# Running maximum in two groups for the dispatch softmax, idle matmuls between the logits' steps, and a table turned by copies

## The chip, the cores and the metric

One core of a Trainium2 chip runs the whole program. The metric is the device time of one execution in microseconds (us); lower is better. Engines are called PE (TensorE's matmuls; PEld is its weight loads), DVE (VectorE), ACT (ScalarE), POOL (GpSimd) and SP (the queue from which nearly all DMAs are issued).

## The reference

Three stages follow one another. x has 8 batches of 3072 tokens of 256 numbers, 24576 tokens in all.

```python
def _attn_ref(x):                       # x: (8, 3072, 256)
    X = np.fft.fft(x, axis=1)
    X = np.fft.fft(X, axis=2)
    return X.real.astype(np.float32)

def _moe_ref(x, phi, w1, w2):           # x: (24576, 256), phi: (256, 32)
    logits = x @ phi
    d = np.exp(logits - logits.max(0, keepdims=True))     # dispatch softmax, over tokens
    d /= d.sum(0, keepdims=True) + 1e-09
    slot_input = d.T @ x                                  # 32 slots
    ...                                                   # 8 experts of 4 slots: relu(s @ w1) @ w2
    c = np.exp(logits - logits.max(1, keepdims=True))     # combine softmax, over slots
    c /= c.sum(1, keepdims=True) + 1e-09
    return c @ slot_out

def _moe2_ref(x, w_in, w_out, s, b):
    r = np.maximum(x @ w_in, 0.0)
    return (s * (r * r) + b) @ w_out
```

The change concerns `logits`, `d` and the sum `d.T @ x`. The maximum over tokens, one number for each of the 32 slots, only keeps the exponentials in range: any common factor of a slot's column of `exp` is divided out again by the sum below it.

## The kernel before

The program is one stream of instructions for each engine, in the order in which the Python code emits them; each engine works through its own stream in order and waits at semaphores that the framework sets. Memory that holds 1 MB blocks is cut into pages: a ring of 15, and 5 more once the first stage is over (`page`, `drop`, `more_pages`). The helper `pump` emits the next pending loads (`todo`) as soon as the count of free pages allows; on the chip SP then waits until the last reader of that page is done. `ORDER` is the order of the first loads: x blocks (`x`), second-layer weights (`w`), the logits' tables (`l`, `ltab_load`), the transform's tables (`h`, `htab_load`) and the x pages that the sum `d.T @ x` reads (`r`, `load_xr`).

The first stage projects the turned x on phi and does one part of the Fourier transform. It leaves `tt`. Then come the parts that the change touches, in this order:

- **Logits** (lines 561 to 592). 16 chunks in two halves `h` that sit in the lower and upper 64 rows. The loop runs 9 steps `st`; a step does one chunk of each half (the first and the last step one chunk only). One chunk is 8 matmuls in the code, 16 records in the trace, into a PSUM tile `lp`, of which there are six. ACT copies `lp` to `lg` (L583). DVE takes the maximum over the chunk's 16 entries of each slot out of `lp` into a column of `cm` (L585).
- **Maximum over tokens** (lines 588 to 611). DVE folds the columns of `cm` (L589, L592), PE turns the result (L598), DVE reduces it over the rows (L603) and spreads it on a diagonal (L605), PE multiplies by ones (L607), DVE copies the result to `cmb` (L608). PE runs idle matmuls on `ones` beside it (`keep_warm`, L190). Two pending steps of the second-layer weights (L216) are emitted here too, by `side_step`; the page `wo` is dropped after the last of them. `fill_stack` (L534 to L536) makes six small copies on ACT.
- **Transform of the weights** (lines 613 to 670). 16 chunks `i`. `emit_d` subtracts `cmb` from the logits (L633, odd chunks on POOL, even ones on DVE), ACT takes the exponential (L669), PE does 4 matmuls against the tables `htab_t` (L652; 8 records of 104 columns on 128 weight columns), and `h_out` copies each chunk's result to `hh` (L643), one half on ACT and the other on DVE.
- **Sum over tokens** (lines 675 to 862). For each of 14 steps PE turns `hh` (L704), multiplies by a DFT table (L712), and adds `d.T @ x` into `racc` (L727). Each part drops the x page that it has read, and `pump` loads another page there: the rest of x, then the second-layer input weights and the experts' weights w1 and w2. After that the experts run, and at some 238 us the last stage starts, which lasts to the end.

Each half of a transform table is loaded twice (L352): into rows 0 to 47 and into rows 64 to 111. `htab_clear` (L357) then clears what each copy must not hold.

Of the kernel before, what the change touches and what calls it, by code (L numbers as in the profile page):

```python
# [32 lines left out]
def tile_fft2__then__softmoe__then__act_relu2(  # L33
# [18 lines left out]
    nc = tc.nc  # L52
# [244 lines left out]
    ORDER = "xxxwxxxxxxwxxxxxxwxxxxwxrllhhrr"  # L297
# [48 lines left out]
    def htab_load(i):  # L346

        t, k = page([R, 16, 2, 4 * MH], F32, "htab_t")
        htabs.append((t, k))
        nc.gpsimd.memset(t[32:64], 0.0)  # L350
        for q in range(2):
            nc.sync.dma_start(out=t[64 * q:64 * q + M], in_=htab[:, 32 * i:32 * i + 32].rearrange("r (k q) m -> r k q m", q=2))  # L352
        dma_ready(2.5)
# [172 lines left out]
    cmb = keep.tile([P, NE], F32, name="cmb")  # L526
# [25 lines left out]
    temps = tc.alloc_tile_pool(name="temps", bufs=1, side="right")  # L552
    cm = temps.tile([R, NCH + 1, NE], F32, name="cm")
    cm1 = temps.tile([R, NE], F32, name="cm1")
    def lgf(i):
        return lg[i // 4][:, 4 * (i % 4):4 * (i % 4) + 4].rearrange("p k g e -> p (k g) e")

    with tc.tile_pool(name="ps_l", bufs=6, space=PSUM) as psl, \
            tc.tile_pool(name="ps_m", bufs=1, space=PSUM) as psm:
        mxp[:] = [psm, 1]  # L560
        done_l = 0
        for st in range(NCH // 2 + SKEW):
            halves = [(h, st - SKEW * h) for h in range(2) if 0 <= st - SKEW * h < NCH // 2]
            lps = {h: psl.tile([R, KC, NG * NE], F32, name="lp") for h, _ in halves}
            for k in range(2 * KC):
                q = P // 2 * (k % 2)
                m = M if q else P // 2
                for h, i8 in halves:
                    r = slice(64 * h, 64 * h + 64)
                    nc.tensor.matmul(  # L570
                        lps[h][q:q + m, k // 2, :], lhsT=ltabs[i8 // 4][0][r, 2 * KC * (i8 % 4) + k, 0:m],
                        rhs=tt[r, 2 * KC * i8 + k].rearrange("p b e -> p (b e)"), start=True, stop=True,
# [27 lines left out]
        while side_step(0.0, True):  # L600
            pass
# [708 lines left out]
```

## Time and profile before

| | us |
|---|---|
| median of 3 runs | 1400.3 |
| lowest and highest run | 1399.29, 1404.01 |
| the profiled execution, span | 1411.6 |

A profile is of one more execution, with the profiler on. All stretches in this document are in us from the start of that execution's span, on its own clock; the span is 11.3 us over the median of the unprofiled runs. A profile's page gives the share of busy time of each engine, the TensorE clock that was granted (in tenths of full speed, in 40 slices of the span), the chain of work that ended last, and groups of instructions by line. Other views give busy times by stretch, instructions in order of time, and who waited for whom.

### The profile page before, as it was taken

The page shows a single profiled execution, that of the slowest core. Times are in us where ns is not written, and L with a number is a line of the kernel's source. Part 1 is how long each engine was busy: PE and PEld are TensorE (multiplying, and loading weights), DVE is VectorE, ACT ScalarE, POOL GpSimd, SP SyncE. Part 2 cuts the span into 40 slices and gives each one's busy share as a digit, 9 for nine tenths or more (in the row PEclk, how much of TensorE's full clock was granted, in tenths as well). Part 3 has the DMA queues.
Part 4 walks back from the last instruction along what each step waited for, and adds up shares of the span by engine and source line. Part 5 has one row for each costly group of instructions (what it writes and reads, how often), then busy time and mean ns, then how long its engine had stood idle before and what let it go on. Part 6 is the DMA issues. An engine that isn't in the chain of part 4 may idle for free.

```text
span 1411.6 us, 23102 instructions
## 1 busy us (share of the span) xinstructions
PE 1388.2 (98%) x9036; PEld 856.0 (61%) x9036; DVE 1171.9 (83%) x1490; ACT 1010.7 (72%) x1423; POOL 233.1 (17%) x287
## 2 busy tenths in 40 slices
PE   8989999999999999999999999999999999999998
PEld 5669564566666666666666666666666666666665
DVE  1565764998989999999989898989898989888886
ACT  2774314877777777777877787877777777777775
POOL 1143400021212121211112121111111111111110
PEclk9995999999999999999999999999999999999999
DMA  8995795101010101101010101010101010101001
GB/s 352 414 311 229 291 414 225 29 27 36 20 36 23 36 24 29 30 23 32 23 36 21 34 23 36 23 33 23 36 23 36 23 36 23 33 23 36 23 20 30
DMA packets 72381, 112.27 MB, mean 80 GB/s; under 512 B 33904, under 2 KB 59632, under 8 KB 64976
## 3 DMA queue, kind: packets, MB, share of 16 engines
q1 hardware_dynamic: 72144, 110.70, 23.1%
q8 instruction: 71, 1.16, 0.3%
q14 instruction: 38, 0.31, 0.1%
q0 software_dynamic: 128, 0.10, 0.0%
HBM read 78.48 MB, written 25.17 MB: 73 GB/s over the span
## 4 chain that ended last, share of the span: by engine, by line
PE 88%; DMA 2%; DVE 1%; issue 1%; SPq 0%; ACT 0%; POOL 0%; DVEq 0%; ACTq 0%; POOLq 0%
PE op L1151 46%; PE op L1154 23%; PE fhp L1121 12%; PE racc L727 3%; DMA w2t<-in_moe_w_dram 2%; PE hp L652 2%; PE dps L712 1%; PE lp L570 1%; SPq L1084 0%; DVE cm L585 0%; DVE r L1127 0%; DVE rhl L1112 0%; PE eop L957 0%; DMA g<-gs 0%; PE gp L1055 0%
## 5 line engine op out<-in xcount | busy, mean ns | idle before, releaser
L1151 PE MATMUL op<-whl,rhl 128*128 128x512 f16 x3072 | 1025.3, 379 | 0.8 <-ACT rhl L1111 0.6
L1154 PE MATMUL op<-whl,rhl 128*128 128x256 f16 x3072 | 835.7, 273 | 0.0
L1126 ACT ACTIVATE r<-fhp,wsc 128x768 f32<-128x768 f32 (+1 forms) x513 | 461.8, 900 | 230.0 <-PE fhp L1121 228.8
L1127 DVE SCALAR_TENSOR_TENSOR r<-fhp,r 128x768 f32<-128x768 f32 (+1 forms) x513 | 488.9, 953 | 113.6 <-ACT r L1126 104.0
L1112 DVE TENSOR_TENSOR rhl<-r,rhl 128x768 f16<-128x768 f32 x511 | 506.9, 992 | 0.9 <-ACT rhl L1111 0.9
L1151 PEld LDWEIGHTS <-rhl 128*128 128x128 f16 x3072 | 300.5, 98 | 335.4 <-ACT rhl L1111 0.9
L1111 ACT CAST rhl<-r 128x768 f16<-128x768 f32 x511 | 420.1, 822 | 1.8 <-DVE r L1127 1.8
L1154 PEld LDWEIGHTS <-rhl 128*128 128x128 f16 x3072 | 300.6, 98 | 62.7 <-issue 0.3
L1166 POOL TENSOR_TENSOR ot<-ot,bias 128x256 f32<-128x256 f32 x189 | 138.1, 731 | 974.2 <-DVE ot L1164 974.2
L1121 PE MATMUL fhp<-ct,g 128*128 128x384 f16 x1024 | 250.4, 326 | 1.1 <-DMA g<-gs 0.8
L1121 PEld LDWEIGHTS <-g 128*128 128x128 f16 x1024 | 99.9, 98 | 69.0 <-issue 1.1
L1163 ACT ACTIVATE o<-op,small 128x256 f32<-128x256 f32 x189 | 90.0, 477 | 16.7 <-PE op L1154 16.7
L1164 DVE SCALAR_TENSOR_TENSOR ot<-op,small,o 128x256 f32<-128x256 f32 x192 | 91.7, 478 | 0.3
L394 PE MATMUL vt<-xb,phd 128*64 128x384 f32 (+3 forms) x288 | 49.0, 477 | 5.3 <-DMA xb<-in_x_turned_dram 5.3
L727 PE MATMUL racc<-xrt,dh 128*64 128x256 f32 x384 | 44.5, 383 | 0.4 <-DVE dh L717 0.4
L394 PEld LDWEIGHTS vt<-xb,phd 128*64 128x64 f32 x288 | 26.5, 139 | 25.5 <-issue 13.8
L727 PEld LDWEIGHTS racc<-xrt,dh 128*64 128x64 f32 x384 | 26.3, 137 | 20.9 <-issue 4.5
L419 DVE COPY v<-vq 128x512 f32<-128x512 f32 (+1 forms) x15 | 8.3, 593 | 33.9 <-PE vq L415 33.9
L406 ACT COPY vts<-vt 128x512 f32<-128x512 f32 (+1 forms) x16 | 8.5, 533 | 32.1 <-PE vt L394 32.0
L464 ACT COPY tt<-tps 32x512 f32<-32x512 f32 x48 | 27.7, 577 | 4.9 <-PE tps L450 4.4
L652 PE MATMUL hp<-htab_t,dt 112*128 112x104 f32 x128 | 27.6, 422 | 0.2 <-ACT dt L669 0.2
L652 PEld LDWEIGHTS hp<-htab_t,dt 112*128 112x128 f32 x128 | 27.4, 333 | 0.5 <-issue 0.5
(229 smaller groups left out, 518.0 us busy)
## 6 DMA issues: line engine op xcount, KB each, us to landing
xb<-in_x_turned_dram SPq DMA_DIRECT2D x24, 1024.0 KB, 20.1
xrt<-in_x_pages_dram SPq DMA_DIRECT2D x24, 1024.0 KB, 13.9
out_dram<-ot SPq DMA_DIRECT2D x128, 128.0 KB, 1.7
w1t<-in_moe_w_dram SPq DMA_DIRECT2D x8, 1024.0 KB, 13.7
out_dram<-ot SPq DMA_DIRECT2D x128, 64.0 KB, 2.0
raw<-in_moe_w_out_dram SPq DMA_DIRECT2D x4, 1024.0 KB, 20.3
raw<-in_moe_w_in_dram SPq DMA_DIRECT2D x4, 1024.0 KB, 7.8
w2t<-in_moe_w_dram SPq DMA_DIRECT2D x4, 1024.0 KB, 17.8
```

What stands on the lines that cost most here:

```text
L652: nc.tensor.matmul(hp[q][:, k, :], start=True, stop=True, lhsT=dt.rearrange("p k g e -> p (k g e)")[:, 128 * (2 * k + q):128 * (2 * k + q) ...
L727: nc.tensor.matmul(raccs[acc][64 * h:64 * h + 64, :], lhsT=dh[:, m, g].rearrange("p j e -> p (j e)"), rhs=xr[k][0][:, g, t, :], start=(sum ...
L1111: nc.scalar.copy(a, r2)
L1112: nc.vector.tensor_tensor(out=l, in0=r2, in1=a, op=ALU.subtract)
L1121: nc.tensor.matmul(hp[k * split][:, k, :].rearrange("p (s b m) -> p s b m", s=2, b=B), lhsT=g16[:, f * P:(f + 1) * P], rhs=c, start=True, ...
L1126: nc.scalar.activation(out=r[:, k], in_=hp[i][:, k], func=AF.Relu, scale=wsc[:, 2, p:p + 1])
L1127: nc.vector.scalar_tensor_tensor(out=r2[:, k], in0=hp[i][:, k], scalar=0.0, in1=r[:, k], op0=ALU.max, op1=ALU.mult)
L1151: nc.tensor.matmul(op.rearrange("p h d -> p (h d)"), lhsT=a, rhs=w.rearrange("p h d -> p (h d)"), start=(f == 0), stop=False)
L1154: nc.tensor.matmul(op[:, 0, :], lhsT=l, rhs=w[:, 0, :], start=False, stop=(f == NFC - 1))
L1163: nc.scalar.activation(out=o1, in_=op[:, 1, :], func=AF.Copy, scale=qv)
L1164: nc.vector.scalar_tensor_tensor(out=ot, in0=op[:, 0, :], scalar=qv, in1=o1, op0=ALU.mult, op1=ALU.add)
L1166: nc.gpsimd.tensor_tensor(out=ot, in0=ot, in1=bias, op=ALU.add)
```

## The change

- Logits: after every step's matmuls PE runs three idle matmuls of 128x128 into a tile `warm` of their own (`keep_warm(warm, 3)`, six records). DVE no longer reduces each chunk out of PSUM: once both halves of a pair of chunks are in `lg`, one reduction takes the maximum of the 32 entries of each slot out of `lg`, in steps of 32 numbers. It is emitted behind the copy of the upper half, so there are 8 reductions in place of 16, of twice the length.
- The maximum over tokens is taken twice, by `top(g, step)`. Group 0 covers the first three pairs (chunks 0 to 5 of the transform) and is worked out beside logits' steps 3 to 5: PE's two parts of it stand in PE's stream behind the matmuls of steps 4 and 5. Group 1 covers everything; its steps stand behind the last reduction and behind the first two chunks of the transform. Chunks 0 to 5 subtract the first maximum, the others the second. `fac` = exp(first maximum - second), and two multiplications on POOL scale the part of `hh` that comes from chunks 0 to 5.
- The transform follows the logits directly. The results of chunks are copied out in pairs, with the table index innermost; two of the pairs go to DVE alone. `fill_stack` moves into the transform. Its working memory `dt` becomes two pages, `scr`, which are dropped at the end of the transform. The two pending steps L216 are no longer emitted here; they come up in the sum's loop, from its step 6 on.
- The second copy of a transform table no longer comes by DMA: POOL copies one half across rows and clears the rest.
- `ORDER` has the logits' tables ahead of the first x page.

The diff, cut:

```diff
-    ORDER = "xxxwxxxxxxwxxxxxxwxxxxwxrllhhrr"
+    ORDER = "xxxwxxxxxxwxxxxxxwxxxxwxllrhhrr"
...
         nc.gpsimd.memset(t[32:64], 0.0)
-        for q in range(2):
-            nc.sync.dma_start(out=t[64 * q:64 * q + M], in_=htab[:, 32 * i:32 * i + 32].rearrange("r (k q) m -> r k q m", q=2))
+        nc.gpsimd.memset(t[64:64 + M, :, 0], 0.0)
+        nc.sync.dma_start(out=t[0:M], in_=htab[:, 32 * i:32 * i + 32].rearrange("r (k q) m -> r k q m", q=2))
...
     def htab_clear(i):
-        for q in range(2):
-            nc.gpsimd.memset(htabs[i][0][64 * q:64 * q + M, :, 1 - q], 0.0)
+        t = htabs[i][0]
+        nc.gpsimd.tensor_copy(t[64:64 + M, :, 1], t[0:M, :, 1])
+        nc.gpsimd.memset(t[0:M, :, 1], 0.0)
...
+    GA, ND = 3, 7
+    scr = [page([R, 4, KC, NG, NE], F32, "scr") for _ in range(2)]
...
+    def emit_d(i):
+        dts[i] = scr[i % ND // 4][0][:, i % ND % 4]
+        (nc.gpsimd if i in (0, 1, 2, 3) or i > 4 and i % 2 else nc.vector).tensor_tensor(
...
+            in1=cmb[i >= 2 * GA][:R].unsqueeze(1).to_broadcast([R, 16, NE]),
...
+    def top(g, step):
+        if step == 0:
+            nc.vector.tensor_reduce(out=cmr[g], in_=cm[:, 0:NCH // 2 if g else GA].rearrange("p i e -> p e i"), axis=AX.X, op=ALU.max)
+        elif step == 1:
+            top_t.append(psm.tile([P, P], F32, tag="tps", name="mt")[0:NE, 0:R])
+            nc.tensor.transpose(top_t[g], cmr[g], ident[:R, :R])
+        elif step == 2:
+            nc.vector.tensor_reduce(out=cm2[:, g:g + 1], in_=top_t[g], axis=AX.X, op=ALU.max)
+            nc.vector.tensor_scalar(out=dg[g], in0=ident[:NE, :NE], scalar1=cm2[:, g:g + 1], scalar2=None, op0=ALU.mult)
+        elif step == 3:
+            top_b.append(psm.tile([P, P], F32, tag="tps", name="mb")[:, 0:NE])
+            nc.tensor.matmul(top_b[g], lhsT=ones[:NE, :], rhs=dg[g], start=True, stop=True)
+        else:
+            nc.vector.tensor_copy(cmb[g], top_b[g])
+            if g:
+                nc.vector.tensor_tensor(out=dfa, in0=cm2[:, 0:1], in1=cm2[:, 1:2], op=ALU.subtract)
...
+    for st in range(NCH // 2 + SKEW):
...                                         (the step's matmuls, as before)
+        if st in (GA + 1, GA + 2):
+            top(0, 2 * (st - GA) - 1)
         keep_warm(warm, 3)
...
+            nc.scalar.copy(dst, lp)
+            if h:
+                nc.vector.tensor_reduce(out=cm[:, i8, :], in_=lg[i8 // 2][:, 8 * (i8 % 2):8 * (i8 % 2) + 8].rearrange("p k g e -> p e (k g)"),
+                                        axis=AX.X, op=ALU.max)
+        if st in (GA + 1, GA + 2):
+            top(0, 2 * (st - GA))
+        if st == GA:
+            top(0, 0)
+        if st == GA + 2:
+            for i in range(4):
+                emit_d(i)
+    top(1, 0)
+    emit_exp(0)
+    emit_exp(1)
+    emit_d(4)
+    emit_d(5)
...
-        while side_step(0.0, True):
-            pass
...
-        for i in range(-3, NCH + 1):
+        for i in range(NCH + 1):
...                                         (chunk i's four matmuls)
+            if i < 2:
+                top(1, 2 * i + 1)
+                top(1, 2 * i + 2)
+            if i == 3:
+                fp = psm.tile([P, P], F32, tag="tps", name="fp")[:, 0:1]
+                nc.tensor.matmul(fp, lhsT=rep.rearrange("p r e -> p (r e)"), rhs=dfa, start=True, stop=True)
+            if i > NCH - 2:
+                h_out(i - 1, 1)
+            elif i > 0 and i % 2 == 0:
+                h_out(i - 2, 2)
+            if 5 < i + 5 < NCH:
+                emit_d(i + 5)
...
+            if i + 2 < NCH:
+                emit_exp(i + 2)
+            if i == 3:
+                nc.scalar.activation(out=fac, in_=fp, func=AF.Exp)
+                fill_stack()
+            if i in (7, 11):
+                hq = hh[i // 11].rearrange("p m (c k) -> p m c k", c=2)[:, :, :, 0:2 * KC * GA]
+                nc.gpsimd.tensor_scalar(out=hq, in0=hq, scalar1=fac, scalar2=None, op0=ALU.mult)
+    for _, k_ in scr:
+        drop(k_)
```

## Rows read from the trace of the kernel before

**Rows 1.** The page: span, and the granted clock in 40 slices of 35.3 us.
```profile
span 1411.6 us, 23102 instructions
PEclk9995999999999999999999999999999999999999
```

**Rows 2.** Stretches: length, busy (count) of PE PEld DVE ACT POOL, clock, DMA share, GB/s.
```profile
90.20:95.00 4.80, 4.58 (x124) 4.11 (x125) 2.68 (x5) 4.52 (x9) 3.78 (x4) 1.00 1.05 199
95.00:98.90 3.90, 0.02 (x3) 0.01 (x3) 1.70 (x3) 0.42 (x1) 3.63 (x6) 0.70 0.97 322
98.90:103.40 4.50, 4.50 (x85) 4.50 (x88) 2.00 (x4) 2.15 (x4) 1.75 (x3) 0.50 1.02 422
103.40:107.40 4.00, 3.97 (x70) 3.38 (x62) 3.69 (x6) 2.05 (x4) 0.00 (x0) 1.00 1.01 418
107.40:111.00 3.60, 1.42 (x9) 1.18 (x9) 2.85 (x7) 1.46 (x7) 0.00 (x0) 0.89 1.01 414
111.00:114.50 3.50, 3.33 (x17) 3.06 (x16) 2.56 (x3) 1.90 (x4) 3.05 (x2) 0.50 1.02 424
114.50:142.20 27.70, 27.65 (x130) 27.67 (x131) 10.96 (x22) 13.96 (x29) 7.97 (x7) 0.50 0.40 161
142.20:144.40 2.20, 2.20 (x9) 1.78 (x8) 1.60 (x3) 0.59 (x1) 1.11 (x2) 0.51 0.48 108
144.40:148.00 3.60, 3.19 (x34) 1.67 (x35) 2.66 (x6) 1.64 (x3) 1.99 (x2) 1.00 0.54 228
```

**Rows 3.** The chain that ended last: start, length, what.
```profile
114.55 27.61 PE hp L652 x128
...
222.48 9.61 DMA w2t<-in_moe_w_dram
232.13 1.93 PE eop L957 x26
```

**Rows 4.** Stretches of L570 alone, then of L190 alone: PE, PEld, clock.
```profile
91.40:93.80 2.40, 2.40 (x94) 2.40 (x92) 1.00 1.05 195
99.00:103.30 4.30, 4.30 (x84) 4.30 (x87) 0.50 1.01 417
...
6.50:8.60 2.10, 2.10 (x19) 2.10 (x20) 1.00 0.71 293
...
111.40:114.20 2.80, 2.80 (x16) 2.67 (x15) 0.50 1.02 421
```

**Rows 5.** DVE by line and shape, 90 to 143: count, busy us, mean ns.
```profile
L585 DVE TENSOR_REDUCE cm<-lp 112x32 f32<-112x512 f32 x16 | 10.1, 684 | 7.8 <-ACT lg L583 7.6
L643 DVE COPY hh<-hp 128x208 f32<-128x208 f32 x16 | 8.4, 522 | 17.5 <-PE hp L652 17.5
L633 DVE TENSOR_TENSOR dt<-lg,cmb 112x512 f32<-112x512 f32 x8 | 6.4, 814 | 0.0
...
L589 DVE TENSOR_REDUCE cm<-cm 112x32 f32<-112x384 f32 x1 | 0.8, 814 | 0.0
...
L592 DVE TENSOR_REDUCE cm<-cm 112x32 f32<-112x160 f32 x1 | 0.4, 424 | 0.0
```

**Rows 6.** ACT and POOL by line and shape, 90 to 143.
```profile
L669 ACT ACTIVATE dt<-dt 112x512 f32<-112x512 f32 x15 | 9.3, 627 | 0.4 <-POOL dt L633 0.4
...
L583 ACT COPY lg<-lp 112x512 f32<-112x512 f32 x15 | 7.8, 599 | 6.4 <-PE lp L570 6.3
...
L633 POOL TENSOR_TENSOR dt<-lg,cmb 112x512 f32<-112x512 f32 x8 | 11.0, 1383 | 25.3 <-ACT hh L643 14.6 <-DVE cmb L608 10.7
```

**Rows 7.** Stretches, as rows 2: the last two numbers are DMA share and GB/s.
```profile
122.00:142.00 20.00, 20.00 (x96) 19.99 (x96) 8.05 (x16) 10.41 (x22) 6.18 (x5) 0.50 0.18 68
142.00:156.00 14.00, 13.35 (x109) 7.88 (x108) 11.19 (x23) 6.11 (x11) 9.74 (x10) 0.92 0.55 189
156.00:232.00 76.00, 75.18 (x677) 42.53 (x676) 41.63 (x64) 14.72 (x22) 6.06 (x7) 1.00 0.99 395
```

**Rows 8.** What SP waited for, 55 to 240: total us, times, longest.
```profile
SPq L326 <- PE hp L652: 31.0, 2, 17.7
```

More of the change, by code (lines that the diff above doesn't have):

```diff
@@ L525, in tile_fft2__then__softmoe__then__act_relu2 @@
     stack = keep.tile([P, 2, 64], F32, name="stack")
-    cmb = keep.tile([P, NE], F32, name="cmb")
+    cmb = [keep.tile([P, NE], F32, name=f"cmb{g}") for g in range(2)]
     rm = keep.tile([R, 8, 16], F32, name="rm")
@@ L613, in tile_fft2__then__softmoe__then__act_relu2, with lgc @@
-    temps.release()
+    cm = scr[1][0][:, 3].rearrange("p k g e -> p (k g) e")
+    tmp = tabp.tile([P, 16, NE], F32, tag="tab", name="tmp")
+    cmr = [tmp[0:R, g] for g in range(2)]
+    dg = [tmp[0:NE, 2 + g] for g in range(2)]
+    cm2 = tmp[0:NE, 4]
+    dfa, fac = tmp[0:NE, 5, 0:1], tmp[:, 6, 0:1]
+    rep = tmp[0:NE, 8:12]
+    nc.gpsimd.tensor_copy(rep, ident[:NE, :NE].unsqueeze(1).to_broadcast([NE, 4, NE]))
+    def lgc(i):
+        return lg[i // 4][:, 4 * (i % 4):4 * (i % 4) + 4]
+    dts = {}
@@ new lines, in tile_fft2__then__softmoe__then__act_relu2 @@
+    top_t, top_b = [], []
+    psw = tc.alloc_tile_pool(name="ps_w", bufs=1, space=PSUM)
+    warm = psw.tile([P, P], F32, name="warm")
+    psl = tc.alloc_tile_pool(name="ps_l", bufs=6, space=PSUM)
+    for st in range(NCH // 2 + SKEW):
+        halves = [(h, st - SKEW * h) for h in range(2) if 0 <= st - SKEW * h < NCH // 2]
+        lps = {h: psl.tile([R, KC, NG * NE], F32, name="lp") for h, _ in halves}
+        for k in range(2 * KC):
+            q = P // 2 * (k % 2)
+            m = M if q else P // 2
+            for h, i8 in halves:
+                r = slice(64 * h, 64 * h + 64)
+                nc.tensor.matmul(
+                    lps[h][q:q + m, k // 2, :], lhsT=ltabs[i8 // 4][0][r, 2 * KC * (i8 % 4) + k, 0:m],
+                    rhs=tt[r, 2 * KC * i8 + k].rearrange("p b e -> p (b e)"), start=True, stop=True,
+                    tile_position=(64 * h, q), skip_group_check=True,
+                )
+        if st in (GA + 1, GA + 2):
+            top(0, 2 * (st - GA) - 1)
+        keep_warm(warm, 3)
+        for n, (h, i8) in enumerate(halves):
+            if h and i8 % 4 == 3:
+                drop(ltabs[i8 // 4][1])
+            lp = lps[h]
+            busy("dve", 0.55)
+            at["pe"] += 1.06
+            dst = lg[i8 // 2][:, 8 * (i8 % 2) + h:8 * (i8 % 2) + 8:2].rearrange("p k g e -> p k (g e)")
+            nc.scalar.copy(dst, lp)
[9 more added lines that the diff above has]
+                emit_d(i)
@@ L614, in tile_fft2__then__softmoe__then__act_relu2 @@
+    top(1, 0)
[3 more added lines that the diff above has]
+    emit_d(5)
+    psl.release()
+    psw.release()
     tpool.release()
@@ L617, in tile_fft2__then__softmoe__then__act_relu2, with h_out @@
     hh = [(hpool if q else hpool0).tile([P, 2 * MH, P], F32, name=f"hh{q}") for q in range(2)]
[L618 to L621 removed]
     pst = tc.alloc_tile_pool(name="ps_t", bufs=2, space=PSUM)
[L624 to L639 removed]
+    with tc.tile_pool(name="ps_h", bufs=2, space=PSUM) as psh:
+        def h_out(i, n):
+            o = 4 * (i % 2)
```

106 lines of the change are left out of this document (17 added, 89 removed).

## The prediction, made before the changed kernel ran

> **What bounds the kernel now.** I began with the page: the granted clock is full in all slices but one, the fourth [rows 1], which is where the logits end and the transform begins. The chain of waits says that this place counts: 27.6 us of it are the transform's matmuls, back to back [rows 3]. The table of stretches then shows what goes on there [rows 2]. From 95.0 to 98.9 PE stands still in the middle of the logits, and the clock drops to its lower level, 1.2 of 2.4 GHz; it is back by 103.4, when PE has worked through logits without a pause. From 107.4 to 111.0 PE works 1.42 of 3.60 us, waiting for the maximum, and the clock drops again. The idle matmuls and the transform that follow keep PE busy from 111.0 to 142.2 without a pause, and yet the clock stays at 0.50 for all of it; it rises only around 144.4, once the turns and DFT matmuls of the sum run. So what PE does in the transform does not raise the clock. Whether it is high or low there is decided before the transform begins.
>
> Behind it the bound changes hands. The sum over tokens is set by PE until about 204, then the experts wait for the last weights, which land at 232.1 [rows 3]. DMA runs at 0.99 from 156 to 232, but only at 0.18 and 0.55 in the two stretches before [rows 7]: there it has no free page, since SP waits for the transform to end (31.0 us in two waits) [rows 8]. So time won before 142.2 counts twice, for PE and for the pages, and must be counted on both. The last stage, from 238 on, is untouched.
>
> **The logits' steps.** At full clock 94 records of logits take 2.40 us, at the low one 84 take 4.30 [rows 4]: 0.026 and 0.051 us each, so 0.8 and 1.65 us for a step of 32. Idle matmuls of 128x128 take 2.10 us for 19, 0.11 each [rows 4]; six add 0.66 us at full clock and, as an estimate from the same ratio, 1.3 at the low one. Nine steps from 90.25 end at about 104 if nothing waits, against 105.4 now.
>
> But something does wait. The maximum now comes out of `lg` in SBUF, 1024 entries, 32 numbers apart. The nearest rows are the reductions of `cm`, also in SBUF and also 32 numbers apart: 384 entries in 0.814 us, 160 in 0.424 [rows 5], so 1.74 ns an entry and 0.14 us fixed, which makes 1.92 us. The other bound is the present reduction out of PSUM, 512 entries in 0.684 us [rows 5]: 1.37 us for twice that. I take 1.92, the row of the same memory and the same step. The Trainium skill speaks for that end and against the change: "Advanced Engine Details and Errata", section SBUF Cachelines, says that accesses which each fall into another 16-byte line pay a penalty. The price here is from the rows of `cm`.
>
> DVE is then slower than PE: 1.92 against 1.5 us a step. The first reduction can begin at about 94.0 (two steps, two copies of 0.6 on ACT [rows 6], and the casts that ACT still has to do there). The third ends at 99.6, the fold of three columns (96 entries, 0.31) at 99.9. PE reaches the turn of that maximum at about 97.3 and stands still for some 2.6 us, with everything behind it in its stream. It gets through the logits at 107.2 and the idle matmuls at 107.9; the last copy is done at 108.0, the last reduction, behind the one before it, at 111.0, the fold of eight columns (256 entries, 0.59) at 111.6.
>
> **The place where PE waits.** ACT's first exponentials (half of 0.627 each [rows 6]) allow the transform's first chunk at 108.4, six us earlier than 114.55 [rows 3]. The four subtractions on POOL, 1.05 to 1.4 us each [rows 6], begin when the first maximum is there, at about 105, and are in time. After one chunk, at 109.3, PE's next instruction is the turn of the second maximum, which is there at 111.6. No idle matmul covers these 2.3 us; with the reduction at 1.37 us they would be 0.6. This is the present wait in a new place: there PE did 1.42 us of work in 3.60 and the clock fell [rows 2]; here it does one chunk and some tenths of idle matmuls in as long a stretch.
>
> **The transform.** Its cadence is 27.61 / 16 = 1.73 us a chunk at the low clock [rows 3]. Copies of pairs, exponentials (0.63) and subtractions stay under that: per pair ACT has 1.25 us of exponentials and 0.5 to 1.0 of copy (L643 by count of entries, as a lower bound, or twice 0.522 [rows 5]), against 3.4. `fill_stack` fits in the same room, and so do the scalings on POOL (1248 entries, at most 3.4 us by POOL's row [rows 6]). All of it is hidden at the low clock. If the clock falls in the 2.3 us, chunk 1 begins at 111.8 and 15 chunks take 25.9 us, with some tenths for the small matmuls between: the end is 138.2. If it already falls in the first wait of 2.6 us, some logits' steps run at 2.95 in place of 1.5 us; two of them move it to about 140, as DVE's backlog then shrinks. I take 139, 3.2 us ahead of 142.2.
>
> **Tables and pages.** Half of the transform's tables less (0.64 MB) and the logits' tables one page earlier end the slow stretch of DMA (199 GB/s [rows 2]) some 3 us sooner. Nobody on the path waits for this; should the pause at 95.0 come back, PE would stand in it instead of in the wait at 97.3, so it costs little. POOL's copies take the place of clears. On the other side, `scr` holds two pages until the transform's end and the `wo` page is held until the sum's sixth step. Ten x pages are loaded before the transform ends, in place of 13, and 34 MB remain after it in place of 31. At 395 GB/s [rows 7] three more MB take 8.0 us. The room for them is DMA's idle time from 142 to 156, 0.45 x 14 = 6.3 us [rows 7]. Net the weights land 1.7 us later against the transform's end than now; between minus 1 (if the spare room behind 156 serves too) and plus 8 (if the pages come too late for the idle time).
>
> **The sum.** 3.2 us from the transform's end, less 1.7 us for the pages, plus up to 0.6 us that the experts now stand waiting: some 2.2 us. The profiled execution would go from 1411.6 to 1409.4; I take the same microseconds off the median of the runs, 1400.3, and forecast 1398.
>
> **Rivals.** *The clock holds.* This is what the idle matmuls are there for. For it: PE's pauses would have to be short, and they are if the reduction costs 1.37 us, as out of PSUM; it could also hold through 2.3 us, since the falls in these rows stand behind a pause of 3.9 us and a stretch with 2.2 idle of 3.6 [rows 2]. Against it: the rows of `cm`. Then a chunk takes half of 1.73 us, 0.86, and 15 chunks 13 us; with about 1.4 us for ACT's small copies, the second maximum and pairs that wait, the end is 126.2, 16 us earlier. Less 1.7 us, plus 0.9 us because the sum starts at full clock (2.20 us of it run at the low one [rows 2]): 15.2 us, 1385. With the cheap reduction too it would be 1382.
>
> *The clock holds, but the transform does not halve.* In it PE loads as many weight columns as it streams. The trace speaks against this: 0.11 us for a load and a matmul of 128 columns at full clock, 2.80 / 16 = 0.175 for 112 columns at the low one [rows 4]; loads scale too. The rule behind it is in the Trainium skill, "TensorE: Matmul & The Clock Gate", section LDWEIGHTS, which divides the columns by 1.2 GHz whatever the clock: an estimate by it is 0.15 us a record and 1.2 a chunk. With a chunk between 0.86 and 1.73, at 1.2, the end would come 5 us later than in the rival before: 1390.
>
> *Slower: the clock is low from the logits on.* The idle matmuls then work against the change, at 1.3 us a step, and each low step takes 1.45 us more. For it: the clock did fall in the logits, at 95.0 to 98.9 [rows 2]. Against it: plain logits at the low clock brought it back within 4.5 us [rows 2]. The gain of 3.2 us is gone after three such steps, partly paid by DVE's waits; with all nine the transform starts at 118 and ends at 146, 3.8 us later than now, and with the pages' 1.7 us that is 1405.8.
>
> **How the numbers follow.** The forecast has a chance of 0.57, with a range of its own of 1394 to 1401. The clock holds: 0.30. It holds without halving: 0.03. Low from the logits on: 0.06. The rest, 0.04, is pages that come much too late or a wait that I have not seen. For 8 in 10 the range reaches down to 1382, since the second case is too likely to leave out, and up to 1402. Within 0.3% (4.2 us, about what a measurement of this kernel tells from no change) lies most of the forecast's own range. Faster: 0.30 + 0.03 + 0.11 of the forecast's = 0.44. Same: 0.48. Slower: 0.08.
>
> **What would show it.** In the changed kernel's profile: the reduction of 112x32 from 112x1024 at 1.9 us (or 1.4); PE idle some 2.5 us ahead of both turns of a maximum, ended by DVE; the transform's matmuls beginning near 108; its clock, 0.50 or 1.00, and with it 1.7 or 0.86 us a chunk; three x loads at its end in SP's queue, and DMA near 1.0 right behind it. I am wrong if the clock stays full through the wait after the first chunk, or if the end of the weights does not follow the end of the transform.

## The result, and the profile after

The changed kernel takes 1418.7 us (median of four executions, 1417.33 to 1420.99) against 1400.3 for the kernel before (three executions, 1399.29 to 1404.01): a ratio of 1.0135, with a 95% interval of 1.0113 to 1.0156. It is slower by 18.4 us, and outside the predicted range. One execution of the kernel before beside these (2407.11 us) and one of e10 below (2421.31 us, mean clock 0.556) were far slower than all others, and no median or ratio here contains them.

The profiled execution of the changed kernel took 1420.99 us; its span is 1419.2. In all executions that follow, profiled or not, the time is the span plus 1.7 to 1.9 us, and the profiled one is the fastest of its kernel in seven runs and the slowest in three. So the profiler costs nothing that can be seen here.

The page, as [rows 1]: the span, and the granted clock in 40 slices of 35.5 us.

```profile
span 1419.2 us, 23117 instructions
PEclk9997899999999999999999999999999999999999
```

The stretches, with the columns of [rows 2]: length, busy (count) of PE, PEld, DVE, ACT and POOL, clock, DMA share, GB/s.

```profile
92.90:99.40 6.50, 4.41 (x87) 3.53 (x87) 5.48 (x8) 6.26 (x14) 5.04 (x5) 1.00 1.00 221
99.50:108.10 8.60, 8.60 (x168) 7.18 (x168) 4.43 (x3) 5.08 (x9) 4.66 (x7) 1.00 1.01 409
108.10:109.70 1.60, 0.06 (x1) 0.06 (x2) 1.57 (x3) 1.07 (x2) 0.00 (x0) 1.00 1.02 425
109.70:118.10 8.40, 7.96 (x140) 6.68 (x140) 6.87 (x7) 3.22 (x6) 3.13 (x3) 1.00 0.58 244
119.10:120.25 1.15, 1.13 (x8) 0.97 (x8) 1.15 (x2) 1.15 (x3) 1.15 (x2) 1.00 0.78 164
120.25:121.90 1.65, 0.01 (x1) 0.00 (x0) 1.62 (x3) 0.68 (x2) 0.95 (x1) 1.00 0.99 417
121.90:123.30 1.40, 1.39 (x11) 1.28 (x11) 0.96 (x3) 0.36 (x1) 0.00 (x0) 1.00 0.30 123
123.30:148.30 25.00, 25.00 (x116) 24.71 (x116) 12.13 (x16) 10.14 (x26) 14.57 (x8) 0.50 0.12 43
```

The logits run from 99.5 to 118.1 and the transform from 119.1 to 148.3. PE stands still twice, at 108.1 and at 120.25. Behind the second stand, after one more chunk and the second maximum's small product, the clock falls at 123.3 and stays at 0.50 to the end of the transform. What ended the two stands is in PE's instructions in order of time (start, us, line, the idle time before in brackets):

```profile
88.49 4.38 PE L395 MATMUL vt<-xb,phd 128*64 128x384 f32 x20 [5.51 <-DMA xb<-in_x_turned_dram]
...
109.64 0.27 PE L589 MATMUL mt<-ident,tmp 112*32 112x112 f32 x1 [1.54 <-DVE tmp L586]
...
121.92 0.27 PE L589 MATMUL mt<-ident,tmp 112*32 112x112 f32 x1 [1.66 <-DVE tmp L586]
```

Both are the turns of a maximum, waiting for DVE's fold. DVE's reductions come before it, by line and shape as in [rows 5]:

```profile
L630 DVE TENSOR_REDUCE scr<-lg 112x32 f32<-112x1024 f32 x8 | 15.2, 1948 | 6.0 <-POOL htab_t L357 4.5 <-ACT lg L628 1.5
```

So the wait, the fall of the clock and its price came where the prediction had put them. Two things did not: the logits begin at 99.5, 9.2 us later than in the first profile of before, of which 5.51 us are PE's wait for the last x block (first row above); and the kernel before does not usually pay for a low clock in this place, as the first run below shows.

### The profile page after: what moved, and what is told of

Same layout as the page of the kernel before. It is cut to its first block, busy times and chain, and to the rows that moved or that the text cites. A ratio compares the mean times of both kernels' runs of the same rounds, so it can differ in the third digit from the quotient of the medians.

```text
span 1419.2 us, 23117 instructions
## 1 busy us (share of the span) xinstructions
PE 1390.6 (98%) x9057; PEld 855.0 (60%) x9057; DVE 1176.0 (83%) x1479; ACT 1006.8 (71%) x1415; POOL 246.0 (17%) x294
## 4 chain that ended last, share of the span: by engine, by line
PE 88%; DMA 8%; DVE 2%; SPq 0%; POOL 0%; ACT 0%; issue 0%; DVEq 0%; ACTq 0%
PE op L1180 46%; PE op L1183 23%; PE fhp L1150 12%; DMA xb<-in_x_turned_dram 6%; PE racc L755 3%; DMA w2t<-in_moe_w_dram 2%; PE hp L668 2%; DVE scr L630 1%; PE dps L740 1%; PE vt L395 1%; DVE r L1156 0%; SPq L1113 0%; DVE rhl L1141 0%; POOL bias L276 0%; PE tps L451 0%
## 5 line engine op out<-in xcount | busy, mean ns | idle before, releaser
L395 PE MATMUL vt<-xb,phd 128*64 128x512 f32 (+3 forms) x288 | 50.1, 484 | 11.6 <-DMA xb<-in_x_turned_dram 11.6
L668 PE MATMUL hp<-htab_t,scr 112*128 112x104 f32 x128 | 26.7, 405 | 0.1
L668 PEld LDWEIGHTS hp<-htab_t,scr 112*128 112x128 f32 x128 | 26.0, 315 | 0.4 <-ACT scr L578 0.3
```

The lines of the kernel that those rows point to most:

```text
L395: nc.tensor.matmul(vt[64 * h:64 * h + 64, o:o + k, :], lhsT=phd[:, c, sg, :], rhs=turned(pg, c, i, k, rev), start=(c == 0 and m < 2), stop ...
```

## The experiments

Theory after the result: the profile of before that the prediction rests on shows an unusual execution, so the low clock in the transform is a price that only the change pays regularly, brought by the wait for the second maximum; and the order of loads costs a few us more. The rivals are that the clock falls for another reason, such as the transform's own matmuls or the idle ones, or that the table's copies delay something. Each ratio is against the kernel before on the same chip, in the same set of runs (medians of 1398.9 to 1400.5 us), with its 95% interval. The sets ran on different chips, so runs of two sets are best compared by their ratios.

| run | us | ratio | transform in its profile: us, clock |
|---|---|---|---|
| e1_before | 1399.81 | 1.0002 [0.9987, 1.0018] | 14.57, full |
| the change | 1418.7 | 1.0135 [1.0113, 1.0156] | 29.2, low from 123.3 |
| e2_order_back | 1414.33 | 1.0103 [1.0082, 1.0124] | 29.9, low but for its start |
| e3_tables_back | 1420.05 | 1.0141 [1.0111, 1.0171] | 29.9, low but for its start |
| e4_both_back | 1415.24 | 1.0108 [1.0083, 1.0132] | 29.6, low but for its start |
| e5_order_alone | 1401.66 | 1.0011 [1.0000, 1.0023] | 14.9, full but for 0.9 us |
| e7_cover | 1406.68 | 1.0046 [1.0029, 1.0063] | 18.9, full |
| e8_after_cover | 1417.72 | 1.0128 [1.0109, 1.0146] | 26.9, low from 134.0 |
| e9_before_no_idle | 1413.42 | 1.0095 [1.0080, 1.0110] | 27.6, low |
| e10_corr_act | 1408.46 | 1.0076 [1.0053, 1.0098] | 18.4, full |
| e11_late_turn | 1405.91 | 1.0059 [1.0040, 1.0077] | 18.8, full |
| e13_best_idle | 1402.41 | 1.0025 [1.0012, 1.0037] | 16.5, full |
| e12_best_no_idle | 1411.63 | 1.0099 [1.0079, 1.0119] | 28.5, low from 109.9 |
| e14_early_exp | 1414.86 | 1.0101 [1.0079, 1.0123] | 28.0, low from 116.3 |
| e15_two_idle (executions of two kinds) | 1411.92 | 1.0063 [1.0033, 1.0092] | 16.5, full in this one |
| e16_one_idle | 1411.27 | 1.0077 [1.0050, 1.0104] | 27.8, low from 111.3 |
| e17_two_idle_cover | 1400.94 | 1.0003 [0.9991, 1.0016] | 16.5, full |
| e18_one_idle_cover | 1401.14 | 1.0006 [0.9992, 1.0021] | 16.5, full |

### The kernel before, once more

e1_before is the kernel before without an edit.

> The kernel before, unchanged, profiled once more. Theory 1: the execution that was profiled first was not a typical one; in most executions of this kernel the transform (L652) runs at the full clock. Then the span here is 1397 to 1402 us, the mean clock 0.99 or more, and a chunk of the transform takes 0.85 to 1.1 us in place of 1.73. Theory 2: the 11 us between the first profile's span and the median are what profiling costs. Then the span is again 1409 to 1413 us with the clock at 0.984, beside runs of 1400.

Stretches of its profiled execution, which took 1403.99 us:

```profile
103.80:110.00 6.20, 4.73 (x134) 3.92 (x128) 6.10 (x11) 5.09 (x10) 0.24 (x1) 1.00 1.01 419
110.00:111.10 1.10, 0.61 (x4) 0.29 (x4) 1.10 (x2) 0.00 (x0) 0.00 (x0) 0.51 0.98 410
111.10:114.40 3.30, 3.30 (x19) 3.26 (x18) 2.47 (x5) 1.46 (x7) 0.00 (x0) 0.50 1.02 422
114.40:116.90 2.50, 2.50 (x14) 2.24 (x13) 1.02 (x4) 0.00 (x0) 0.23 (x1) 0.51 1.00 413
116.90:118.50 1.60, 1.43 (x15) 1.26 (x13) 1.60 (x2) 0.80 (x3) 1.60 (x2) 1.00 1.00 410
118.50:133.10 14.60, 14.55 (x128) 14.44 (x128) 10.86 (x22) 14.20 (x31) 9.24 (x7) 1.00 0.66 259
```

The same 128 records of the transform that took 27.61 us in [rows 3] take 14.6 here. The clock falls at 110 as it did there, but idle matmuls and the maximum's two small matmuls fill PE until 118.5, and the clock is back at 116.9, ahead of the transform. In the first profile the transform began at 114.55 [rows 3], 4.3 us after the fall at 110.2, and the clock did not come back in it.

The difference, 13.0 us, is what set that execution apart: 1411.6 - 13.0 + 1.8 = 1400.4, the median. In 82 timed executions of the kernel before beside these runs, none lies outside 1395.5 to 1404.8; the first profile, at about 1413.4 by the same 1.8, lay outside all of them. The mean clock says the same: 0.984 in the first profile, 0.990 to 0.999 in all 82. The profile of e1 is not a typical execution either: it is the slowest of its ten, and the one with 0.990. So the fall of its clock ahead of the transform need not be the usual course; the full clock in the transform is.

### The idle matmuls of the kernel before

e9_before_no_idle takes out its 19 idle matmuls around the maximum:

```diff
-        keep_warm(warm, 8)
...
-        keep_warm(warm, 3)
...
-        keep_warm(warm, 8)
```

> The kernel before without its 19 idle matmuls around the maximum. Theory (they are what brings the clock back ahead of the transform in its typical executions): the clock falls in the maximum's chain and stays low through the transform, which takes 27 to 28 us as in the first profiled execution of before, and the time is 1411 to 1414. Rival (they matter little, and the first profile's low clock was chance): the transform takes about 14.6 us, and the time is 1398 to 1401.

```profile
103.50:107.90 4.40, 0.95 (x11) 0.29 (x6) 4.37 (x9) 1.73 (x7) 0.00 (x0) 1.00 1.01 419
107.90:111.30 3.40, 0.63 (x2) 0.50 (x3) 2.54 (x7) 0.95 (x5) 1.11 (x1) 0.51 1.01 422
111.30:138.90 27.60, 27.58 (x129) 27.60 (x130) 12.11 (x22) 15.43 (x32) 9.91 (x8) 0.50 0.54 213
```

PE works 0.95 us of 4.40, the clock falls at 107.9, and the transform takes 27.60 us, the length in the first profile of before. All four executions lie at 1411.3 to 1414.6 us. So the level of the clock when the transform begins is worth 13 us of the whole time, and in the kernel before the idle matmuls secure it: by their times and clocks in all 82 executions above, though not in the one that was profiled first.

### Order and tables

e2_order_back is the change with the old `ORDER`; e3_tables_back has both copies of the tables by DMA again (and the old clears); e4_both_back has both; e5_order_alone is the kernel before with the new order only.

```diff
-    ORDER = "xxxwxxxxxxwxxxxxxwxxxxwxllrhhrr"
+    ORDER = "xxxwxxxxxxwxxxxxxwxxxxwxrllhhrr"
```

```diff
-        nc.gpsimd.memset(t[64:64 + M, :, 0], 0.0)
-        nc.sync.dma_start(out=t[0:M], ...)
+        for q in range(2):
+            nc.sync.dma_start(out=t[64 * q:64 * q + M], ...)
```

> The changed kernel with the order of the first loads of the kernel before (an x page ahead of the logits' tables). In the changed kernel's trace PE waits 5.5 us for the last x block and the logits begin at 99.5 in place of 90.3. Theory A, the order did it: the logits begin at 90 to 91 and the time falls by 8 to 10 us, to about 1409.5; the clock still falls ahead of the transform. Theory B, the tables that come into rows 0 to 47 alone did it: the logits begin no earlier than 95 and the time stays above 1414.

> The changed kernel with both copies of each transform table loaded by DMA again, and cleared as before; the order of loads stays the changed one. Theory A (the order of loads delays the last x block): no change, 1417 to 1420, the logits still begin near 99. Theory B (tables that come into the lower rows alone): the logits begin at 91 to 94 and the time is 1410 to 1413.

> The changed kernel with the order of loads and the tables' DMAs both as before; only the two maxima, the idle matmuls, the page use and the copies by pairs are left of the change. Theory A and B both give the logits' start back: 90 to 91, and 1409 to 1410 us, since the clock falls behind the transform's first chunk as in the changed kernel and the transform ends near 139. If the transform holds the full clock here, the time is 1396 to 1398.

> The kernel before with the change's order of loads alone (both logits' tables ahead of the page of x). Theory (the order makes the last x land later in front of the logits and nothing makes up for it): 1403 to 1406, the logits starting 4 to 9 us after 90.3. Rival (before's own logits already start as late as 96.9 in one of its executions, so the order is not what costs): 1399 to 1401.

With the old order 4.4 us go away (e2), or 4.8 with the old tables too (e4 against e3), though the intervals overlap; the expectations of e2 and e4, about 1409.5 us, were missed. With the old tables nothing goes away (e3 and e4 differ from the runs without that edit by +1.4 and +0.9 us, inside their intervals). In the kernel before, the new order alone costs 1.6 us (0 to 3.2), nearer to the rival's 1399 to 1401 than to the theory's 1403 to 1406. The reason can be seen in the DMA rate around 77 us, of the change and then of e2, the change with the old order:

```profile
77.00:80.00 3.00, 3.00 (x18) 1.62 (x18) 2.41 (x4) 2.94 (x6) 1.65 (x2) 1.00 1.08 231
80.00:84.00 4.00, 2.98 (x21) 1.98 (x17) 1.65 (x2) 2.91 (x6) 0.00 (x0) 1.00 1.03 186
84.00:88.00 4.00, 0.00 (x0) 0.00 (x0) 2.10 (x3) 0.75 (x2) 0.00 (x0) 0.72 1.01 163
```

```profile
77.00:80.00 3.00, 3.00 (x21) 2.03 (x18) 2.62 (x3) 2.91 (x6) 0.06 (x1) 1.00 1.00 404
80.00:84.00 4.00, 3.88 (x31) 2.39 (x30) 1.76 (x4) 2.83 (x6) 0.00 (x0) 1.00 1.07 223
84.00:88.00 4.00, 3.30 (x80) 2.90 (x80) 3.85 (x8) 3.91 (x9) 0.67 (x1) 1.00 1.06 169
```

While the tables load, the engines of the DMA are busy all the time but move only 160 to 230 GB/s, against some 400. In the new order this slow stretch begins some 3 us earlier, and the last x block is then still under way. It does not end sooner, as the prediction had it: in the change the rate from 96 to 100 us is still 254 GB/s, with the old order 416:

```profile
96.00:100.00 4.00, 2.48 (x79) 2.20 (x70) 3.01 (x5) 3.88 (x10) 3.68 (x5) 1.00 0.98 254
```

```profile
96.00:100.00 4.00, 3.86 (x76) 3.02 (x74) 3.52 (x3) 1.95 (x4) 3.76 (x5) 1.00 1.01 416
```

The DMA issues of 60 to 100 us list it with 26.3 us from issue to landing in the change and 20.4 in e2:

```profile
xb<-in_x_turned_dram SPq DMA_DIRECT2D x1, 1024.0 KB, 26.3
```

```profile
xb<-in_x_turned_dram SPq DMA_DIRECT2D x1, 1024.0 KB, 20.4
```

The first stage waits for that block, and the logits for the first stage. The start of the logits also moves from execution to execution (90.3 and 96.9 in two profiles of before), so the 9.2 us between two single profiles overstate the 4.4 us of the timed runs. All profiles together bear the smaller figure out: in the five with the new order (the change, e3, e5, e8, e10) the rate falls under 300 GB/s at 77 to 78 us and the logits begin at 94.3 to 99.8, on average 97.1; in the fourteen with the old order these are 80 to 81, and 89.3 to 96.9, on average 92.3. With all this undone, e4 keeps 15 us, and its transform is at the low clock.

### Covering the wait for the second maximum

e7_cover is e4, and e8_after_cover the whole change, with idle matmuls ahead of the second turn:

```diff
+            if i == 0:
+                keep_warm(psm.tile([P, P], F32, tag="tps", name="warm2"), 7)
```

> The change with the old order of loads and tables by DMA (1415.24 us), and seven idle matmuls queued on TensorE ahead of the second maximum's turn, where it waits some 1.7 us for VectorE. Theory (the clock falls because of that wait, and the transform then runs its 28 to 30 us at the low clock): the granted clock stays at full through the transform, the transform takes 15 to 17 us in place of 29.6, and the time is 1400 to 1403. Rival (it falls for another reason, say the transform's own narrow matmuls or the idle matmuls between the logits): the transform still takes 28 to 30 us and the time is 1414 to 1418.

> The whole change (1418.7 us) with the same seven idle matmuls ahead of the second maximum's turn. Theory: full clock in the transform, 15 to 17 us in place of 29.2, time 1404 to 1407; the order of loads keeps its 4.4 us. Rival: transform 28 to 30 us, time 1417 to 1421.

e7, the stretch from the last logits to the transform's end:

```profile
115.50:119.50 4.00, 3.64 (x31) 3.29 (x30) 3.97 (x4) 2.77 (x6) 3.21 (x3) 1.00 0.75 283
119.50:135.40 15.90, 15.17 (x125) 14.41 (x125) 12.19 (x19) 10.43 (x26) 14.05 (x8) 1.00 0.20 72
```

Seven idle matmuls hold the clock through the whole transform and give back 8.6 us of e4's 15 (1415.24 to 1406.68). The theory holds, its time doesn't: at full clock the transform still takes 18.9 us, and 1400 to 1403 was not reached.

In e8 the clock held past the second turn too, but the time hardly moved. Its clock fell later, at 134.0. What happened there (DVE and POOL, then PE, in order of time):

```profile
126.16 3.80 DVE L571 TENSOR_TENSOR scr<-lg,cmb 112x512 f32<-112x512 f32 x1
...
130.38 5.50 DVE L571 TENSOR_TENSOR scr<-lg,cmb 112x512 f32<-112x512 f32 x1
...
126.37 3.44 POOL L699 TENSOR_SCALAR hh<-hh,tmp 128x1248 f32<-128x1248 f32 x1
129.80 2.52 POOL L571 TENSOR_TENSOR scr<-lg,cmb 112x512 f32<-112x512 f32 x2
132.30 3.43 POOL L699 TENSOR_SCALAR hh<-hh,tmp 128x1248 f32<-128x1248 f32 x1
...
136.44 6.73 PE L668 MATMUL hp<-htab_t,scr 112*128 112x104 f32 x30 [3.89 <-DVE hh L658]
```

A subtraction of DVE takes 0.68 us at its shortest in this run (the one at 118.98). The two here take 3.80 and 5.50, and each ends 0.15 us behind POOL's multiplication of `hh` (126.37 + 3.44 = 129.81 and 129.96; 135.73 and 135.88). DVE's copy of `hh` out of PSUM stands behind each of them; PE waits 3.89 us for the copy behind the second, and the clock falls in the wait. The Trainium skill states such a lock in "SBUF — State Buffer", section "SBUF: two separate sides": a DVE operation with two inputs in SBUF and a GpSimd operation share a pair of ports, and one is blocked for the whole instruction of the other. The rows agree that DVE is held to the end of POOL's instruction. Which of two instructions goes first they don't settle: the first subtraction is recorded 0.21 us ahead of the multiplication that it then waited for, and the second was held through a subtraction of POOL as well as the multiplication.

### The correction on ScalarE, and the turn a chunk later

e10_corr_act is e8 with the two multiplications on ACT:

```diff
-                nc.gpsimd.tensor_scalar(out=hq, in0=hq, scalar1=fac, scalar2=None, op0=ALU.mult)
+                nc.scalar.activation(out=hq, in_=hq, func=AF.Copy, scale=fac)
```

> The whole change with the seven idle matmuls (1417.72 us, transform 26.9 us), and the two corrections of the first group's rows (128x1248 each) moved from GpSimd to ScalarE. Theory (VectorE's subtractions are held while GpSimd works on these corrections, 3.80 and 5.50 us in place of 0.68, TensorE then waits 3.89 us for a copy and its clock falls): no subtraction on VectorE over 1.6 us in the transform's second half, no wait of TensorE over 1 us there, full clock to the end, transform 17 to 19 us, time 1405 to 1410. Rival (the length of these subtractions has another cause): the long subtractions and the wait remain, 1415 to 1420.

The same two subtractions:

```profile
126.62 0.76 DVE L571 TENSOR_TENSOR scr<-lg,cmb 112x512 f32<-112x512 f32 x1
...
128.29 0.78 DVE L571 TENSOR_TENSOR scr<-lg,cmb 112x512 f32<-112x512 f32 x1
```

The held subtractions are gone, the clock is full to the transform's end, and the ratio falls from 1.0128 to 1.0076, about 7 us. What stays is 1.0076, against 1.0046 in e7. These two differ in the order, the tables and the engine of the scalings, and their intervals overlap, so what is left is not split between them here.

e11_late_turn takes e4 and, in place of idle matmuls, turns the second maximum one chunk later; the subtractions of chunks 6 and 7 move behind it.

```diff
-            if i < 2:
-                top(1, 2 * i + 1)
-                top(1, 2 * i + 2)
+            if 1 <= i < 3:
+                top(1, 2 * i - 1)
+                top(1, 2 * i)
```

> The change with the old order of loads and tables by DMA (1415.24 us), with the second maximum turned one chunk of the transform later and no idle matmuls added: its wait shrinks from 1.7 us to about 0.6. Theory (that wait is what brings the clock down): full clock through the transform, 17 to 18.5 us, time 1404 to 1408. Rival (a wait of 0.6 us is still enough, or the clock falls without any wait): transform 28 to 30 us, 1413 to 1417.

```profile
116.70 0.27 PE L588 MATMUL mt<-ident,tmp 112*32 112x112 f32 x1 [0.78 <-DVE tmp L585]
```

1405.91 us, at full clock in the transform, without one added matmul: it is the wait that costs, here shortened to 0.78 us.

### Reductions out of PSUM, and fewer idle matmuls

e13_best_idle is e11 with the corrections on ACT and 16 reductions out of `lp`, as before the change; e12_best_no_idle is that without the idle matmuls of the logits.

```diff
-            if h:
-                nc.vector.tensor_reduce(out=cm[:, i8, :], in_=lg[i8 // 2][...].rearrange("p k g e -> p e (k g)"), ...)
+            nc.vector.tensor_reduce(out=cm[:, 2 * i8 + h, :], in_=lp.rearrange("p k (b e) -> p e (k b)", e=NE), ...)
```

> The same as the run with the later turn, with the corrections on ScalarE and the sixteen reductions out of PSUM as in the kernel before (0.68 us each in place of eight of 1.9). Theory (the SBUF reductions make the two waits, and nothing else of the change costs the path): no wait ahead of either turn, full clock, logits 19 to 20 us as the idle matmuls set them, transform 16 to 17 us, time 1400 to 1404. Rival (the clock still falls): 1412 to 1416.

> The run before this one (reductions out of PSUM, later turn, corrections on ScalarE), without the idle matmuls between the logits. Theory (TensorE is what the logits wait for, and 0.94 us of each of its stages is idle matmuls): logits 14 to 16 us in place of 20, transform 16 to 17 us at full clock, and the time 1396 to 1400, at or under the kernel before. Rival (without them the clock falls between the logits): transform 28 to 30 us, 1408 to 1413.

```profile
L628 DVE TENSOR_REDUCE scr<-lp 112x32 f32<-112x512 f32 x16 | 10.4, 686 | 9.4 <-ACT lg L627 6.6 <-issue 2.7
```

DVE's 16 reductions out of PSUM take 10.4 us, against 15.2 for 8 out of SBUF above. With them, with the corrections (the scalings of `hh`) on ACT and with the later turn 1.0025 is left. Without idle matmuls the logits shrink from 18.8 to 16.0 us, but PE then waits 1.6 us ahead of the transform for ACT's exponential, the clock falls at 109.9, and 9 us are lost: the rival's time, but the clock fell behind the logits and not between them.

Then three runs with the first exponentials issued earlier (`emit_exp(0)` and `emit_exp(1)` in the last step but one), no idle matmuls behind the last logits, and three, two or one of them between the steps.

> The run with PSUM reductions, later turn and corrections on ScalarE (1402.41 us), its first two exponentials issued before the last logits' copies and no idle matmuls behind the last logits. Theory (the 1.46 us between the last logits and the transform are on the path): the gap shrinks to 0.3 us or less, the time to 1400 to 1401.5. Rival (the landing of weights or x sets the end whatever the transform does): no change, 1402 to 1403.

> As the run before this one, with two idle matmuls in place of three between stages of the logits. Theory (idle matmuls are on the path, 0.31 us each in eight stages, and two keep the clock): logits 16 to 17.5 us, full clock in the transform, 1397.5 to 1399.5. Rival (two are too few): the clock falls, transform 28 us, 1409 to 1413.

> As before with one idle matmul between stages. Theory (one is still enough): logits 15 to 16 us, full clock, 1395 to 1398. Rival (too few, as none was): transform 28 us, 1408 to 1413.

```profile
113.00:114.80 1.80, 0.10 (x3) 0.05 (x1) 0.95 (x3) 1.80 (x4) 1.80 (x3) 1.00 0.76 246
114.80:116.30 1.50, 1.50 (x14) 1.50 (x14) 1.50 (x2) 0.24 (x1) 0.80 (x1) 1.00 0.89 366
116.30:142.80 26.50, 26.50 (x123) 25.97 (x122) 10.25 (x19) 13.07 (x28) 7.44 (x6) 0.50 0.17 61
```

These are e14's stretches. Both of its expectations failed: the gap between logits and transform did not shrink, it grew to 1.70 us, and since no idle matmuls lie in it any more, the clock falls. PE goes on at 114.78, 0.1 us after DVE has read the last `lp`, whose pool in PSUM is released just ahead of the transform's own; the profile itself names a subtraction of POOL as the releaser, so which of them held PE is not shown. In e15, with a gap of 1.92 us, executions of one and the same kernel are of two kinds: three at 1398.5 to 1401.7 us with a mean clock of 0.997 to 0.999, seven at 1410.8 to 1415.4 with 0.984 to 0.989. That is about the 13 us by which the transform of the two profiles of before differs. e16, with one idle matmul between the steps and the gap empty too, is of the slower kind in all four of its executions.

e17_two_idle_cover and e18_one_idle_cover put idle matmuls back into that gap alone:

```diff
-        if st < NCH // 2 + SKEW - 1:
-            keep_warm(warm, 2)
+        keep_warm(warm, 2 if st < NCH // 2 + SKEW - 1 else 7)
```

The code shown is e17's; e18 has 1 in place of 2.

> As the run with two idle matmuls between stages, and seven behind the last logits, where TensorE waited 1.92 us. Theory (that wait alone decides): every execution at full clock in the transform, 1397 to 1401.5 us, median about 1399.5. Rival (the thinner stages decide): still executions of both kinds or all slow, median 1405 to 1413.

> As the run with one idle matmul between stages, and seven behind the last logits. Theory (the wait ahead of the transform alone decides): logits and cover 17 us, every execution at full clock, 1396 to 1399. Rival (one is too few to bring the clock through the waits between the logits): 1408 to 1413, or executions of both kinds.

```profile
108.00:109.90 1.90, 1.76 (x15) 1.58 (x15) 1.05 (x3) 1.90 (x5) 1.90 (x3) 1.00 1.02 418
109.90:126.50 16.60, 16.20 (x133) 15.40 (x133) 12.20 (x20) 12.89 (x29) 9.55 (x7) 1.00 0.47 188
```

The transform with one idle matmul between the steps, first in e16 (gap empty) and then in e18 (gap filled):

```profile
109.60:137.40 27.80, 27.80 (x134) 27.27 (x135) 11.75 (x20) 13.27 (x29) 7.61 (x7) 0.53 0.29 116
```

```profile
112.70:129.40 16.70, 16.20 (x133) 15.41 (x133) 12.29 (x21) 12.93 (x29) 8.89 (x7) 1.00 0.49 194
```

With the gap filled, all 11 executions of either kernel lie at 1396.7 to 1404.3 us, with a mean clock of 0.993 or more. What decides is the gap: one idle matmul between the logits' steps is enough once the gap is filled, and too few while it is empty. No run has none between the steps and the gap filled. One does no better than two: e18's logits took 17.3 us, 19.1 with the matmuls in the gap, where 17 for both were expected; PE stood 0.74 us in them with no release that the profile shows. Both kernels equal the kernel before and don't beat it: from the first logits to the transform's end e17 needs 36.1 us (90.34 to 126.46) and e1 needs 36.2 (96.92 to 133.12).

## Why the prediction was wrong

**The base (failed, and the largest term).** The first paragraph took the profiled execution as the kernel's normal course, and the sum took "the same microseconds off the median". That execution was 11.3 us over the median, and its transform ran at the low clock for 27.6 us. Both stood in the rows and were not put together: the profiler costs nothing, and the 13.0 us between 27.6 and 14.6 are the distance. Against a typical execution the forecast's own end of the transform would have been a loss of some 10 us (139 against 142.15 - 13.0 = 129.1). The run of the kernel before alone shows this; e9 shows it from the other side.

Set against e1's profile, the change's span is 17.1 us longer: 2.6 us because the logits begin later (99.47 against 96.92), 12.7 from there to the transform's end (48.9 against 36.2) and 1.6 from there to the weights (91.2 against 89.5). Ahead of the transform the change did gain: it begins 19.65 us after the first logits, against 21.63. Behind the first logits the loss lies in the transform, 29.2 us against 14.6.

**The reductions (right).** 1.92 us forecast, 1.948 measured. The other end, 1.37 us for twice the row out of PSUM, is what e13 measured for two (2 x 0.686). The penalty that the Trainium skill names in "Advanced Engine Details and Errata", section SBUF Cachelines, agrees with these rows in its sign, 0.58 us a reduction. That it is the cause is not shown: no run has the same reduction out of SBUF at another step.

**The waits and the clock (right in place, too long).** 2.6 and 2.3 us were forecast ahead of the two turns, 1.54 and 1.66 came: a step of the logits with its six idle records takes 1.89 us (113.25 to 115.14), not 1.5, so DVE falls less far behind. Both terms of the step were too small: 32 records of logits took 1.02 us in place of 0.8, the six idle ones 0.87 in place of 0.66. The clock fell behind the second, as said; the first, among logits and idle matmuls, didn't bring it down. e7 fills the second wait and e11 shortens it to 0.78 us, and in both the clock stays.

**The transform and the weights (right, in part by luck).** From the first logits to the transform's end 48.75 us were forecast (90.25 to 139) and 48.9 measured. Two misses cancel in this: the transform began 1.5 us later than forecast (19.65 us after the first logits, not 18.15) and took 29.2 us, not 30.6. The weights land 91.2 us behind the transform's end:

```profile
230.14 9.37 DMA w2t<-in_moe_w_dram
```

Against 89.9 in [rows 3] that is 1.3 us more, where 1.7 were forecast for the pages.

**The order (failed).** "Nobody on the path waits for this" overlooked that the tables' slow transfers would now run beside the last x block, which is on the path, and the slow stretch did not end sooner. It cost some 4 us. The `DMA` share told nothing of it, since it is 1.0 at 404 and at 163 GB/s; the rate did.

**"All of it is hidden" (failed where the clock is full).** The scalings on POOL were placed beside the work at the low clock only. At full clock they hold DVE for up to 5.5 us, and PE with it (e8 against e10: about 7 us). In the change itself one subtraction took 3.37 us too, but this is covered, because PE is slow there and never waits (25.00 of 25.00 us busy).

**The rivals.** "The clock holds" had 1385, from the same wrong base. Where it held, with the change's reductions and corrections but the old order and tables (e7, e11), the time was 1406, and at best 1400.9 (e17). That the transform would not halve is refuted: 14.57 / 16 is 0.91 us a chunk at full clock, near the 0.86 worked out from the rows. The estimate of 1.2 from "TensorE: Matmul & The Clock Gate", section LDWEIGHTS, of the Trainium skill doesn't hold here: it added load and matmul, and in e1's transform both were busy nearly all the time (14.44 and 14.55 of 14.60 us). The 128 weight columns are also more than the 104 that are streamed, not as many. The slower rival was the wrong mechanism: the clock stayed full in the logits. A change that is slower because the usual kernel before is faster than its profile had no place among them.

In ratios the loss is accounted for by steps: 1.0135 with everything, 1.0108 with the old order and tables, 1.0059 with the wait shortened, 1.0025 with reductions out of PSUM and corrections on ACT, 1.0003 with a shorter logits stage and the gap covered. The first two intervals overlap, and the last two steps are each of several edits made together, so single edits in them are not separated. What decides in one execution whether a wait of 1.9 us brings the clock down (e15) stays open, and so does PE's standing still in the logits with no visible release (1.86 us in e1, 0.74 in e18).

## What to carry to other kernels

Before a sum is made on a profile, compare its execution's own time with the timed runs; where it lies outside them, look for the stage that makes the difference, and forecast against the usual course. When an engine's stream is rearranged, look for every place where PE has nothing to do just ahead of a long stage, since the clock with which it enters may hold for all of it: turning a maximum one chunk later was worth as much as idle matmuls (e11 and e7). And a transfer that is moved earlier should be set against what is in flight there, by its rate and not by its busy share.

## What the runs showed of the hardware

- A transform of 128 records took 14.6 us at full clock and 27.6 at the low one with PE busy throughout (27.58 of 27.60 in e9). In two profiles (the first of before, e9) the clock was low when the transform began, in eight it fell inside (the change, e2, e3, e4, e8, e12, e14, e16), and in none of the ten did it come back before the transform's end; in the two kernels where this was looked at, it came back once the turns and DFT matmuls of the sum ran (144.4 before, 150.6 in the change). In e5 it was low for the first 0.9 us of the transform and full from there.
- One kernel had executions of two kinds with no difference in its program: in e15 three at 1398.5 to 1401.7 us with a mean clock of 0.997 to 0.999, seven at 1410.8 to 1415.4 with 0.984 to 0.989.
- VectorE's subtraction of two SBUF operands took 3.80 and 5.50 us in place of 0.68 beside GpSimd's operations (e8), and its copies out of PSUM took 0.58 us there as elsewhere in that run.
- The DMA engines were busy at a share of 1.0 while the rate was 163 to 231 GB/s, during the tables' loads, against some 400 before them; the last x block, 1 MB, took 26.3 us from issue to landing where it was under way in this stretch (the change) and 20.4 in e2.
